# Decoder block on one core: TensorE's extra work folded into its loop, loads issued from a loop, heads in groups four apart

## The chip, the core and the metric

One core of one Trainium2 chip. A core has TensorE (PE), VectorE (DVE), ScalarE (ACT), GpSimd (POOL) and SyncE (SP); each runs its own program, and they wait for one another by semaphores. SP here does nothing but issue DMA transfers, which 16 DMA engines carry from the chip's memory (HBM) into the on-chip memory of 128 partitions. The metric is the device time of one execution in microseconds (us), the median of several. A profile is one execution seen by the hardware profiler; its span runs from the first to the last instruction.

## The reference

```python
def _A_ref(x, k_cache, v_cache, wq, wo):          # B, Sq, D = 4, 1, 512; H, Sk, Dh = 32, 4096, 128
    q = (x @ wq).reshape(B, Sq, H, Dh).transpose(0, 2, 1, 3)
    scores = jnp.einsum("bhqd,bhkd->bhqk", q, k_cache) * (Dh ** -0.5)
    p = _softmax(scores, axis=-1)
    o = jnp.einsum("bhqk,bhkd->bhqd", p, v_cache)
    return o.transpose(0, 2, 1, 3).reshape(B, Sq, H * Dh) @ wo
...
def _B_ref(x, w1, w2, w3, w4):                     # F = 1792
...
    x1 = x + hs
    h2 = _gelu(_layernorm(x1, axis=-1) @ w3) @ w4
    return x1 + h2
...
xn = _layernorm(x, axis=-1)
return x + _A_ref(xn, A_k_cache, A_v_cache, A_wq, A_wo) + _B_ref(xn, B_w1, B_w2, B_w3, B_w4)
```

With one position, every shift that builds `hs` moves zeros in, so `hs` is zero, `x1` is its input, and `w1` and `w2` are not read. What is left is attention of one query per head over 4096 cached keys and values (4 batches of 32 heads, float32), and a small MLP.

## The kernel before

K and V are 268 MB each and are read once. The 128 pairs of batch and head are cut into NG = 32 groups of HG = 4. A group's K is 8.39 MB: 128 partitions of 64 KB each, partition p holding 128 key rows of head p // 32 of the group. Before the change a group is four neighbouring heads, one contiguous stretch of memory:

```python
            def group(flat, g):
                n = HG * S * DH
                return flat[g * n:(g + 1) * n].rearrange("(p r) -> p r", p=P)
```

Three slots of 64 KB per partition hold everything large. K alternates between slot 1 (even groups) and slot 0 (odd groups); V has slot 2. Weights use the slots when they are free: wq lies in slot 2 at the start, the MLP's w3 and w4 in slot 2 at the end, wo in slot 0 at the very end. The last V group goes to slot 1.

Per group, four engines work one behind the other.

- DVE (L321 to L340) spreads the group's four queries into `qb`, waits for K, multiplies K by `qb` in two halves (L330, L332), sums the products to 128 scores per partition (L335), gives K's slot free (`k_free`), takes the maximum of each head (L337 to L340) and hands it to ACT (`d_a`).
- ACT (L238) takes exponentials into the tile `pw` and their sums into `rs`, and hands on to PE (`a_p`).
- PE waits for V (`s_v`) and for `pw`, runs 32 matmuls of `pw` with V (32 partitions by 512 columns into `pv`), one that sums `rs`, gives V's slot free (`v_free`), waits until ACT has copied `pv` to `os` (L244), and runs four small ones that collect the outputs into `oz`.
- SP keeps two orders: K of group g+2 behind `k_free` of group g (L119), V of group g+1 behind `v_free` of group g (L136), by turns, in one queue.

At the start x is loaded and normalised on DVE (to L308), PE multiplies it by wq with 32 matmuls, ACT scales the result, DVE transposes it (L316) and copies it to `Q` (L317). Then `d_T` lets SP issue K of group 1 and V of group 0. K of group 0 was issued right behind wq, in two halves (L123); a GpSimd relay passes the second half's arrival to DVE as `s_h`, and gives it 32 tokens at once, so that every turn of DVE's loop can take one.

SP's program has 65 loads written out. PE, ACT and DVE run loops over the groups. PE's and ACT's loops end before the last group, whose V is elsewhere: its turn, the MLP's first layer and the normalised outputs (`spread`: a matmul of a masked copy of each batch's outputs with a 0/1 matrix) are written out behind the loop. When the last reduce has freed slot 0, SP issues wo in six pieces (L148); PE multiplies each as it lands, 24 of the 32 row blocks into `y` and the last eight straight into `total`. Two copies and two stores of 4 rows end the program.

Of the kernel before, what the change touches and what calls it, by code (L numbers as in the profile page):

```python
# [7 lines left out]
F32 = mybir.dt.float32  # L8
AF = mybir.ActivationFunctionType
ALU = mybir.AluOpType  # L10
# [10 lines left out]
def decode_block(ctx: ExitStack, tc: tile.TileContext, x, k, v, wq, wo, w3, w4, out):  # L21
# [26 lines left out]
    X = sbuf("X", [P, WC, B])  # L48
# [3 lines left out]
    mask = sbuf("mask", [P, 4])  # L52
# [7 lines left out]
    ot = sbuf("ot", [P, JB, HG])  # L60
    rec = sbuf("rec", [P, JB, HG])
    lt = sbuf("lt", [P, H, 4])

    pv, oz, total, y, pa, pb = (nc.alloc_psum_tensor(f"ps{i}", [P, 512], F32) for i in range(6))
# [7 lines left out]
    PIECES = ((0, 8), (8, 16), (16, 24), (24, 28), (28, 31), (31, 32))  # L72
    CUT = 24
    s_x, s_v, s_vl, s_kh, s_h = (sem(n) for n in ("sx", "sv", "svl", "skh", "sh"))
    s_wq = [sem(f"swq{n}") for n in range(2)]
    s_k = [sem(f"sk{n}") for n in range(2)]
    s_wo = s_k + [s_v, s_x, s_kh, s_h]
    d_self, g_a, c_done, d_T, k_free, v_free = (sem(n) for n in ("dself", "ga", "cd", "dT", "kf", "vf"))
    d_a, a_d, p_a, a_p, d_p = (sem(n) for n in ("da", "ad", "pa", "ap", "dp"))

    kf = k.rearrange("b h s d -> (b h s d)")
    vf = v.rearrange("b h s d -> (b h s d)")
    out_r = out.rearrange("b s d -> (b s) d")

    def group(flat, g):
        n = HG * S * DH
        return flat[g * n:(g + 1) * n].rearrange("(p r) -> p r", p=P)
# [4 lines left out]
    q_sb = S0[:, 4 * D:6 * D].rearrange("p (n f) -> p n f", n=2)  # L92
    qT = S0[:, 6 * D:8 * D]
    xp = S0[:, 8 * D:8 * D + 2 * P].rearrange("p (e c i) -> p e c i", e=2, c=NC)
    xnT = S0[:, 9 * D:9 * D + P].rearrange("p (c m) -> p c m", c=NC)
    wq_sb = S2[:, :].rearrange("p (c n) -> p c n", c=NC)
    w3_sb = S2[:, :NC * F].rearrange("p (c f) -> p c f", c=NC)
    w34 = NC * F + NF * D
    w4_sb = S2[:, NC * F:w34].rearrange("p (m n) -> p m n", m=NF)
    hs, gu, gt, gT = (S2[:, w34 + n * FT:w34 + (n + 1) * FT] for n in range(4))  # L100
    V3 = S2[:, :].rearrange("p (c d) -> p c d", c=C)
    VL = S1[:, :].rearrange("p (c d) -> p c d", c=C)
# [10 lines left out]

    with tc.tile_critical(no_gpsimd_drain=True), nc.Block(no_gpsimd_drain=True) as block:

        @block.sync
        def _(e):
            def load_k(g):
                e.dma_start(KS[g % 2][:, :], group(kf, g)).then_inc(s_k[g % 2], 16)  # L119

            def load_k_half(g, n, s):
                r = slice(n * ROW // 2, (n + 1) * ROW // 2)
                e.dma_start(KS[g % 2][:, r], group(kf, g)[:, r]).then_inc(s, 16)  # L123

            wq_r = wq.rearrange("(p c) n -> p c n", p=P)
            for n in range(2):
                c = slice(n * NC // 2, (n + 1) * NC // 2)
                e.dma_start(wq_sb[:, c, :], wq_r[:, c, :]).then_inc(s_wq[n], 16)
# [12 lines left out]
            e.dma_start(S1[:, :], group(vf, NG - 1)).then_inc(s_vl, 16)  # L141
            take(e, v_free)
            e.dma_start(w3_sb, w3.rearrange("(p c) f -> p c f", p=P)).then_inc(s_wq[0], 16)
            e.dma_start(w4_sb, w4.rearrange("(p m) n -> p m n", p=P)).then_inc(s_wq[1], 16)
            take(e, k_free)
            wo_r = wo.rearrange("(p c) n -> p c n", p=P)
            for n, (c0, c1) in enumerate(PIECES):
                e.dma_start(wo_sb[:, c0:c1, :], wo_r[:, c0:c1, :]).then_inc(s_wo[n], 16)  # L148

        @block.gpsimd  # L150
        def _(e):
            e.memset(xs, 0.0).then_inc(g_a, 1)
            e.memset(ident[:, :], 0.0).then_inc(c_done, 1)
            e.memset(rs[:, :], 0.0)
            e.memset(pw[:, :, :], 0.0).then_inc(g_a, 1)
# [3 lines left out]
            take(e, s_kh, 16)  # L159
            e.wait_ge(c_done, 2).then_inc(s_h, NG)  # L160

        @block.tensor
        def _(e):
            def contract(V):
                for g in range(G4):
                    t = g % 4
                    i = mm(e, pv[32 * t:32 * t + 32, :], pw[:, g, :], V[:, 4 * g:4 * g + 4, :], g < 4, g >= G4 - 4)
                return i

            def outputs(done):  # L170
                i = mm(e, oz[:, HG:2 * HG], ones[:, :], rs[:, :], True, True)
                if done is not None:
                    i.then_inc(done, 1)
                take(e, a_p)
                for m in range(4):
                    i = mm(e, oz[:, 0:HG], os[:, m, :], sel[:, HG * m:HG * m + HG], m == 0, m == 3)
                i.then_inc(p_a, 1)

            def spread(b):
                take(e, d_p)  # L180
                mm(e, pa[:, 32 * b:32 * b + 32], lt[:, :, :], sel[:, :], True, True).then_inc(p_a, 1)

            e.wait_ge(d_T, 1)
            for c in range(NC):
                if c % (NC // 2) == 0:
                    take(e, s_wq[c // (NC // 2)], 16)
                w = wq_sb[:, c, :].rearrange("p (n j h d) -> p n h j d", n=2, j=JB // 2, h=HG)
                for n in range(2):
                    for h in range(HG):
                        i = mm(e, (pa, pb)[n][32 * h:32 * h + 32, :], xnT[:, c, :], w[:, n, h], c == 0, c == NC - 1)  # L190
                    if c == NC - 1:
                        i.then_inc(p_a, 1)

            with nc.Fori(0, NG - 1, 1, engines=[ET.PE]):
                take(e, s_v, 16)
                take(e, a_p)
                contract(V3).then_inc(p_a, 1)
                outputs(v_free)
            for b in range(B - 1):
                spread(b)  # L200
            take(e, a_p)
            take(e, s_vl, 16)
            contract(VL).then_inc(p_a, 1)
            e.wait_ge(s_wq[0], 16)
            for c in range(NC):
                for t in range(4):
                    i = mm(e, pb[32 * t:32 * t + 32, :FT], x1T[:, c, :], w3_sb[:, c, t * FT:(t + 1) * FT],
                           c == 0, c == NC - 1)
            i.then_inc(p_a, 1)
            outputs(None)  # L210
            spread(B - 1)
            mm(e, total[:, 0:P], ident[:, :], base[:, :], True, False)
            e.wait_ge(s_wq[1], 16)
            e.wait_ge(d_p, 1)
            for m in range(NF):
                t = m % 4
                mm(e, y[32 * t:32 * t + 32, :], gT[:, 32 * m:32 * m + 32], w4_sb[:, m, :], m < 4, False)

        @block.scalar
        def _(e):  # L220
# [5 lines left out]
            for n in range(2):  # L226
                take(e, p_a)
                e.mul(q_sb[:, n, :], (pa, pb)[n][:, :], DH ** -0.5).then_inc(a_d, 1)
            e.wait_ge(d_T, 2)
            e.activation(os[:, 0, 0:1], st[:, 3:4], AF.Exp)  # L230
            take(e, g_a)

            def weights():
# [6 lines left out]
                i.then_inc(a_p, 1)  # L240

            def outputs(o):
                take(e, p_a)
                e.copy(os[:, :, :], pv[:, :].rearrange("p (m d) -> p m d", m=4)).then_inc(a_p, 1)  # L244
# [3 lines left out]
            def spread(b):  # L248
                take(e, p_a)
                return e.copy(X[:, :, b], pa[:, 32 * b:32 * b + 32])  # L250

            with nc.Fori(0, NG - 1, 1, engines=[ET.Activation]) as g:
                weights()
                e.drain().then_inc(a_d, 1)
                outputs(OS[:, bass.ds(g, 1), :])
            weights()
            e.drain().then_inc(a_d, 1)
            for b in range(B - 1):
                spread(b).then_inc(c_done, 1)
            take(e, p_a)  # L260
            e.copy(os[:, :, :], pv[:, :].rearrange("p (m d) -> p m d", m=4)).then_inc(a_p, 1)
            take(e, p_a)
            e.copy(hs.rearrange("p (m i) -> p m i", i=32),
                   pb[:, :FT].rearrange("p (i m) -> p m i", i=32)).then_inc(a_d, 1)
# [159 lines left out]
```

## Time and profile before

| what | value |
|---|---|
| time, median of 3 (lowest to highest) | 1305.07 us (1304.78 to 1305.14) |
| the profiled execution's own time | 1304.94 us |
| its span | 1303.2 us |
| VectorE busy | 1169.3 us, 90% |
| TensorE matmuls busy | 364.8 us, 28% |
| ScalarE busy | 98.9 us, 8% |
| read from HBM | 561.00 MB, 430 GB/s over the span |
| TensorE's mean granted clock | 0.627 of full speed |

An engine's busy share tells which engines are far from a limit, not which one sets the time: the DMA queue is a resource of its own, with its own row. A part of the profile names, for each wait, what ended it; waits on semaphores that ran through the waiting engine's own sequencer appear there as "DVEq" or "PEq". A matmul in float32 appears as two records (x64 for 32 matmuls).

### The profile page before, as it was taken

What the parts mean: (1) busy time and instruction counts of PE and PEld (TensorE: products, weight loads), DVE (VectorE), ACT (ScalarE), POOL (GpSimd) and SP (SyncE); (2) the same over time, 40 slices, a digit from 0 to 9 for tenths busy, and PEclk for the clock granted to TensorE, in tenths of its full rate; (3) what the DMA queues carried; (4) which work ended last, traced back from release to release, by engine and by line L of the source; (5) the groups of instructions that cost most, each with busy time, mean ns of one, the idle gap of its engine ahead of it and who ended that gap; (6) DMA issues with size and microseconds to landing.
All of it is one profiled execution on the core that took longest, in us unless ns stands there. A gap on an engine that the chain in (4) does not pass through costs nothing. (4 is left out here: it accounts for less than half of the span.)

```text
span 1303.2 us, 7027 instructions
## 1 busy us (share of the span) xinstructions
PE 364.8 (28%) x2622; PEld 130.6 (10%) x2622; DVE 1169.3 (90%) x343; ACT 98.9 (8%) x335; POOL 2.1 (0%) x9
## 2 busy tenths in 40 slices
PE   2032123333113333213333212333311333321347
PEld 0010001111001111001111000111000111100112
DVE  4999999999999999999999999999999999999971
ACT  1000000000000000000000000000000000000010
POOL 0000000000000000000000000000000000000000
PEclk9565566666566666566666556666556666655669
DMA  9999999999999999999999999999999999999998
GB/s 403 435 447 422 447 420 449 420 447 422 430 437 424 445 422 447 422 447 422 447 420 449 421 447 422 439 428 428 441 422 447 422 445 424 445 424 445 422 429 347
DMA packets 10830, 561.08 MB, mean 431 GB/s; under 512 B 1212, under 2 KB 1220, under 8 KB 1480
## 3 DMA queue, kind: packets, MB, share of 16 engines
q1 hardware_dynamic: 10808, 561.00, 99.6%
q8 instruction: 3, 0.05, 0.0%
q14 instruction: 3, 0.02, 0.0%
q10 hardware_dynamic: 16, 0.01, 0.0%
HBM read 561.00 MB, written 0.01 MB: 430 GB/s over the span
## 5 line engine op out<-in xcount | busy, mean ns | idle before, releaser
L335 DVE TENSOR_REDUCE sc<-slot 128x128 f32<-128x16384 f32 x32 | 551.0, 17220 | 8.2 <-DVEq L70 8.2
L112 PE MATMUL ps<-slot,pw 128*32 128x512 f32 x2048 | 294.9, 740 | 882.2 <-PEq L70 882.2
L330 DVE TENSOR_TENSOR slot<-slot,qb 128x8192 f32<-128x8192 f32 x32 | 278.1, 8692 | 43.6 <-DVEq L70 43.6
L332 DVE TENSOR_TENSOR slot<-slot,qb 128x8192 f32<-128x8192 f32 x32 | 277.9, 8684 | 2.1 <-DVEq L70 2.1
L112 PEld LDWEIGHTS ps<-slot,pw 128*32 128x32 f32 x2048 | 80.7, 133 | 1071.0 <-issue 1070.9
L238 ACT ACTIVATE pw<-sc,st 32x128 f32<-32x128 f32 x128 | 67.3, 525 | 243.0 <-ACTq L70 241.5
L244 ACT COPY os<-ps 128x512 f32<-128x512 f32 x31 | 18.1, 585 | 857.1 <-ACTq L70 857.1
L112 PE MATMUL ps<-sel,os 128*128 128x4 f32 x256 | 32.8, 252 | 17.5 <-PEq L70 17.5
L112 PEld LDWEIGHTS ps<-sel,os 128*128 128x128 f32 x256 | 31.0, 191 | 19.3 <-issue 19.3
L238 ACT ACTIVATION_READ_ACCUMULATOR pw<-sc,st 32x1 f32 x128 | 26.1, 204 | 0.0
L112 PE MATMUL ps<-slot 128*32 128x512 f32 x92 | 14.0, 747 | 18.8 <-PEq L70 17.6
L327 DVE STREAM_TRANSPOSE qb<-qx 128x128 f32<-128x128 f32 x32 | 10.0, 311 | 4.9 <-DVEq L70 0.5
L386 DVE COPY res<-ps 64x128 f32<-64x128 f32 x1 | 0.3, 283 | 15.2 <-PE ps L112 15.2
L337 DVE TENSOR_REDUCE st<-sc 128x1 f32<-128x128 f32 x32 | 9.2, 286 | 4.7
L356 DVE TENSOR_TENSOR slot<-slot 128x448 f32<-128x448 f32 x1 | 0.6, 624 | 13.1 <-DVEq L70 13.1
L112 PE MATMUL ps<-rs,ones 128*128 128x4 f32 x64 | 12.3, 263 | 0.0
L112 PEld LDWEIGHTS ps<-rs,ones 128*128 128x128 f32 x64 | 9.5, 188 | 26.7 <-issue 26.7
L324 DVE COPY qx<-Q 128x128 f32 x32 | 7.3, 227 | 4.9 <-issue 4.6
L339 DVE STREAM_TRANSPOSE mt<-mx 128x32 f32<-128x32 f32 x32 | 6.8, 211 | 4.7
L340 DVE TENSOR_REDUCE st<-mt 128x1 f32<-128x32 f32 x32 | 6.0, 186 | 4.8 <-DVEq L70 1.8
L338 DVE COPY mx<-st 128x32 f32<-128x32 f32 x32 | 5.8, 181 | 4.7
L246 ACT COPY OS<-ps 128x8 f32 x31 | 5.1, 165 | 42.4 <-ACTq L70 42.4
(58 smaller groups left out, 54.2 us busy)
## 6 DMA issues: line engine op xcount, KB each, us to landing
slot<-in_A_wq_dram SPq DMA_DIRECT2D x2, 4096.0 KB, 16.8
slot<-in_A_k_cache_dram SPq DMA_DIRECT2D x2, 4096.0 KB, 35.8
slot<-in_B_w_dram SPq DMA_DIRECT2D x2, 3584.0 KB, 22.7
slot<-in_A_wo_dram SPq DMA_DIRECT2D x3, 2048.0 KB, 30.1
slot<-in_A_wo_dram SPq DMA_DIRECT2D x1, 1024.0 KB
slot<-in_A_wo_dram SPq DMA_DIRECT2D x1, 768.0 KB, 37.9
slot<-in_A_v_cache_dram SPq DMA_DIRECT2D x32, 28.8
slot<-in_A_k_cache_dram SPq DMA_DIRECT2D x31, 42.3
```

The costliest lines, as they stand in the source:

```text
L112: return e.matmul(o, l, r, start=start, stop=stop)
L238: i = e.activation(o, sc[r, :].rearrange("p (g w) -> p g w", w=4), AF.Exp, bias=st[r, 1:2], scale=1.0, accum_out=rs[r, h:h + 1])
L244: e.copy(os[:, :, :], pv[:, :].rearrange("p (m d) -> p m d", m=4)).then_inc(a_p, 1)
L324: own(e.tensor_copy(qx[:, :].rearrange("p (h r) -> p h r", h=4), Q[:, bass.ds(g + n, 1), :].rearrange("p o h -> p (o h)").unsqueeze(2) .to ...
L327: own(e.transpose(qb[:, :], qx[:, :]))
L330: e.tensor_tensor(out=K[:, :C // 2, :], in0=K[:, :C // 2, :], in1=qw, op=ALU.mult).then_inc(d_self, 1)
L332: e.tensor_tensor(out=K[:, C // 2:, :], in0=K[:, C // 2:, :], in1=qw, op=ALU.mult).then_inc(d_self, 1)
L335: e.reduce_sum(sc[:, :], K, axis=AX.X).then_inc(d_self, 1)
L337: own(e.reduce_max(st[:, 0:1], sc[:, :], axis=AX.X), 2)
L338: own(e.tensor_copy(mx[:, :], st[:, 0:1].to_broadcast([P, 32])))
L339: own(e.transpose(mt[:, :], mx[:, :]))
L340: e.tensor_reduce(st[:, 1:2], mt[:, :], axis=AX.X, op=ALU.max, negate=True).then_inc(d_a, 1)
```

## The change

Four things change, and the placement of TensorE's code.

1. **Heads and loads.** A group is now four heads that lie four apart (head 16n + 4t + e, for t = 0 to 3). Its K or V is four pieces of 2.1 MB, 8.4 MB apart in HBM; a load's source pattern counts 4, then 32, then 16384 elements, and its destination 128 partitions. SP's loads stand in a loop of eight turns with an address from a register.
2. **wq and the last group inside PE's loop.** wq is loaded like a V group into slot 2, and the loop's first of 33 turns multiplies it; DVE puts the normalised x into eight extra columns of `pw` for that. The last V group goes to slot 2 like the others, in two pieces (40 KB and 24 KB per partition); w3 and w4 go to slot 1 ahead of it. In every turn the last 12 matmuls of the 32 wait for a token of `v_rest`, which GpSimd gives out in the manner of `s_h` before.
3. **Outputs by a transpose.** DVE normalises 24 groups, then the last 8, and transposes them into `X`; the masked matmuls and their copies go. wo's rows are ordered to match (source pattern 4, then 32, then a piece of a row), and its pieces are 12, 8, 5, 3, 3 and 1 of 32.
4. **DVE's product** is one instruction over the whole of K, no longer two halves, and K of group 0 is one load.
5. **Code placement.** PE starts with a branch that, by a register, goes once to a block behind its loop and back.

```diff
-    PIECES = ((0, 8), (8, 16), (16, 24), (24, 28), (28, 31), (31, 32))
-    CUT = 24
+    PIECES = ((0, 12), (12, 20), (20, 25), (25, 28), (28, 31), (31, 32))
+    CUT = 28
+    GF = 20
...
+    NB = B * 2
+    kf = k.rearrange("b (n t e) s d -> (b n) e t (s d)", n=2, t=HG).rearrange("m e t (p r) -> m e t p r", p=32)
+    vf = v.rearrange("b (n t e) s d -> (b n) e t (s d)", n=2, t=HG).rearrange("m e t (p r) -> m e t p r", p=32)
...
+    nc.vector.addr_align(128, offset=100, max_nops=0)
+    turn = nc.alloc_registers("pe_turn_of_two", engines=[ET.PE])
+    nc.regs_mov(turn, 0)
...
-            for n in range(2):
-                c = slice(n * NC // 2, (n + 1) * NC // 2)
-                e.dma_start(wq_sb[:, c, :], wq_r[:, c, :]).then_inc(s_wq[n], 16)
-            load_k_half(0, 0, s_k[0])
-            load_k_half(0, 1, s_kh)
-            e.wait_ge(d_T, 2)
-            load_k(1)
-            for g in range(NG - 1):
-                if g > 0:
-                    take(e, v_free)
-                e.dma_start(S2[:, :], group(vf, g)).then_inc(s_v, 16)
-                if g + 2 < NG:
-                    take(e, k_free)
-                    load_k(g + 2)
+            def src(flat, m, i):
+                return flat[m, i] if isinstance(m, int) else flat[bass.ds(m, 1), i].rearrange("m t p r -> (m t) p r")
+            def load_k(m, i):
+                e.dma_start(KS[i % 2][:, :], src(kf, m, i)).then_inc(s_k[i % 2], 16)
+            def load_v(m, i):
+                take(e, v_free)
+                e.dma_start(S2[:, :], src(vf, m, i)).then_inc(s_v, 16)
+            FIRST, REST = slice(0, GF * 4 * DH), slice(GF * 4 * DH, ROW)
+            wq_r = wq.rearrange("(p c) n -> p (c n)", p=P)
+            e.dma_start(S2[:, FIRST], wq_r[:, FIRST]).then_inc(s_v, 16)
+            e.dma_start(S2[:, REST], wq_r[:, REST]).then_inc(s_q, 16)
+            load_k(0, 0)
+            e.wait_ge(d_T, 1)
+            load_k(0, 1)
+            with nc.Fori(0, NB, 1, engines=[ET.SP]) as m:
+                for i in range(3):
+                    load_v(m, i)
+                    take(e, k_free)
+                    if i < 2:
+                        load_k(m, i + 2)
...
-            e.dma_start(S1[:, :], group(vf, NG - 1)).then_inc(s_vl, 16)
-            take(e, v_free)
-            e.dma_start(w3_sb, w3.rearrange("(p c) f -> p c f", p=P)).then_inc(s_wq[0], 16)
-            e.dma_start(w4_sb, w4.rearrange("(p m) n -> p m n", p=P)).then_inc(s_wq[1], 16)
+            e.dma_start(w3_sb, w3.rearrange("(p c) f -> p c f", p=P)).then_inc(s_w3, 16)
+            e.dma_start(w4_sb, w4.rearrange("(p m) n -> p m n", p=P)).then_inc(s_w4, 16)
+            take(e, v_free)
+            last = src(vf, NB - 1, 3)
+            e.dma_start(S2[:, FIRST], last[:, :, FIRST]).then_inc(s_v, 16)
+            e.dma_start(S2[:, REST], last[:, :, REST]).then_inc(s_q, 16)
             take(e, k_free)
-            wo_r = wo.rearrange("(p c) n -> p c n", p=P)
+            wo_r = wo.rearrange("(h q c) n -> q h (c n)", h=H, q=4)
...
+            with nc.body("pe_top", valid_engines=pe):
+                e.br_lt(turn, 1, on_true="pe_far", on_false="pe_near")
+            with nc.body("pe_near", valid_engines=pe):
+                with nc.Fori(0, NG + 1, 1, engines=pe) as g:
+                    e.br_lt(g, NG, on_true="pe_turn", on_false="pe_mlp")
...
+                    take(e, s_v, 16)
+                    take(e, a_p)
+                    for n in range(G4):
+                        if n == GF:
+                            take(e, v_rest)
...
+                nc.br("pe_far", engines=pe)
+            with nc.body("pe_far", valid_engines=pe):
+                nc.regs_alu(turn, turn, 1, op=ALU.add)
+                e.br_lt(turn, 2, on_true="pe_top", on_false="pe_rest")
...
-                    e.tensor_tensor(out=K[:, :C // 2, :], in0=K[:, :C // 2, :], in1=qw, op=ALU.mult).then_inc(d_self, 1)
-                    take(e, s_h)
-                    e.tensor_tensor(out=K[:, C // 2:, :], in0=K[:, C // 2:, :], in1=qw, op=ALU.mult).then_inc(d_self, 1)
+                    own(e.tensor_tensor(out=K, in0=K, in1=qb[:, :].unsqueeze(1).to_broadcast([P, C, DH]), op=ALU.mult))
```

How the instructions stand, at three places. A row names the line, the operation, destination<-source, the destination's shape and the semaphores it waits for. **SP, from its first transfer**, before:

```order
L128 DMA slot<-in_A_wq_dram 128x8192 x2
L123 DMA slot<-in_A_k_cache_dram 128x8192 x2
L119 DMA slot<-in_A_k_cache_dram 128x16384 [waits dT]
L136 DMA slot<-in_A_v_cache_dram 128x16384
L119 DMA slot<-in_A_k_cache_dram 128x16384 [waits kf]
L136 DMA slot<-in_A_v_cache_dram 128x16384 [waits vf]
```

and now (the ISA rows work out addresses):

```order
L126 DMA slot<-in_A_wq_dram 128x10240
L127 DMA slot<-in_A_wq_dram 128x6144
L118 DMA slot<-in_A_k_cache_dram 128x1x16384
L118 DMA slot<-in_A_k_cache_dram 128x1x16384 [waits dT]
L131 UNCONDITIONAL_BRANCH
L122 ISA [waits vf]
L122 DMA slot<-in_A_v_cache_dram 128x1x16384
L118 ISA [waits kf]
L118 DMA slot<-in_A_k_cache_dram 128x1x16384
```

The order of K and V in the queue is the same; the first K is one load, the first V waits too, and a K or V load's destination carries a dimension of one because its source has one more than before. **SP, at the end of the groups**, before:

```order
L136 DMA slot<-in_A_v_cache_dram 128x16384 [waits vf]
L141 DMA slot<-in_A_v_cache_dram 128x16384 [waits kf]
L143 DMA slot<-in_B_w_dram 128x7168 [waits vf]
L144 DMA slot<-in_B_w_dram 128x7168
L148 DMA slot<-in_A_wo_dram 128x4096 [waits kf]
```

and now:

```order
L131 COMPARE_AND_BRANCH
L147 DMA slot<-in_B_w_dram 128x7168
L148 DMA slot<-in_B_w_dram 128x7168
L151 DMA slot<-in_A_v_cache_dram 128x1x10240 [waits vf]
L152 DMA slot<-in_A_v_cache_dram 128x1x6144
L156 DMA slot<-in_A_wo_dram 128x1x6144 [waits kf]
```

w3 and w4 have moved ahead of the last V group; the wait for `kf` that stood before that group's load is now the last one inside the loop. **PE, from its first matmul through one turn of its loop**, before:

```order
L112 MATMUL ps<-slot 32x512 [waits swq0,dT]
L112 MATMUL ps<-slot 32x512 x15
L112 MATMUL ps<-slot 32x512 [waits swq1]
L112 MATMUL ps<-slot 32x512 x15
L194 UNCONDITIONAL_BRANCH
L112 MATMUL ps<-slot,pw 32x512 [waits sv,ap]
L112 MATMUL ps<-slot,pw 32x512 x31
L112 MATMUL ps<-rs,ones 128x4
```

and now:

```order
L180 COMPARE_AND_BRANCH
L105 MATMUL ps<-slot,x1T 32x448 [waits sw3]
L105 MATMUL ps<-slot,x1T 32x448 x15
L188 UNCONDITIONAL_BRANCH
L105 MATMUL ps<-slot,pw 32x512 [waits sv,ap]
L105 MATMUL ps<-slot,pw 32x512 x19
L105 MATMUL ps<-slot,pw 32x512 [waits vr]
L105 MATMUL ps<-slot,pw 32x512 x11
L105 MATMUL ps<-rs,ones 128x4
```

The 32 matmuls with wq have gone into the loop's own 32; the MLP's 16 stand in the loop under a branch that only the last turn takes.

More of the change, by code (lines that the diff above doesn't have):

```diff
@@ L59, in decode_block @@
     res = sbuf("res", [2 * 32, 2, P])
[L60 to L64, printed above, removed]
+    ot = sbuf("ot", [P, B, H])
+    rec = sbuf("rec", [P, NG, HG])
+    warm = sbuf("warm", [P, 1])
+    pv, oz, total, y, pb = (nc.alloc_psum_tensor(f"ps{i}", [P, 512], F32) for i in range(5))
     def sem(name):
@@ new lines, in load_v @@
+            def load_v(m, i):
[11 more added lines that the diff above has]
+                    load_v(m, i)
+                    take(e, k_free)
+                    if i < 2:
+                        load_k(m, i + 2)
+                e.br_lt(m, NB - 1, on_true="sp_more", on_false="sp_next")
+                with nc.body("sp_more", valid_engines=[ET.SP]):
+                    after = nc.s_assert_within(m + 1, None, NB - 1,
+                                               skip_runtime_bounds_check_because="the last turn skips this block")
+                    load_k(after, 0)
+                    load_v(m, 3)
+                    take(e, k_free)
+                    load_k(after, 1)
+                    nc.br("sp_next", engines=[ET.SP])
+                nc.switch_bb("sp_next")
@@ L158, in _ @@
                             pattern=[[-1, P]], channel_multiplier=1).then_inc(c_done, 1)
-            take(e, s_kh, 16)
-            e.wait_ge(c_done, 2).then_inc(s_h, NG)
+            take(e, s_q, 16)
+            e.wait_ge(c_done, 2).then_inc(v_rest, NG)
+            take(e, s_q, 16)
+            e.wait_ge(c_done, 2).then_inc(v_rest, 1)
         @block.tensor
         def _(e):
[L164 to L168, printed above, removed]
@@ L183, in _ @@
[L183 to L192, printed above, removed]
@@ L194, in _ @@
[L194 to L217, printed above, removed]
+            pe = [ET.PE]
+            nc.br("pe_top", engines=pe)
+            with nc.body("pe_top", valid_engines=pe):
+                e.br_lt(turn, 1, on_true="pe_far", on_false="pe_near")
@@ L225, in _, with values @@
                 e.activation(st[:, 2:3], st[:, 1:2], AF.Sqrt, bias=st[:, 3:4], scale=1.0 / D).then_inc(a_d, 1)
-            for n in range(2):
+            def values():
                 take(e, p_a)
[L228 to L231, printed above, removed]
+                return e.copy(os[:, :, :], pv[:, :].rearrange("p (m d) -> p m d", m=4)).then_inc(a_p, 1)
+            values()
+            e.drain().then_inc(a_d, 1)
+            take(e, p_a)
+            e.activation(warm[:, :], st[:, 3:4], AF.Exp)
             def weights():
@@ L240, in weights @@
                 i.then_inc(a_p, 1)
+                e.drain().then_inc(a_d, 1)
             def outputs(o):
-                take(e, p_a)
-                e.copy(os[:, :, :], pv[:, :].rearrange("p (m d) -> p m d", m=4)).then_inc(a_p, 1)
+                values()
                 take(e, p_a)
                 return e.copy(o, oz[:, 0:2 * HG].unsqueeze(1))
[L248 to L252, printed above, removed]
+            act = [ET.Activation]
@@ L253, in _ @@
+            with nc.Fori(0, NG, 1, engines=act) as g:
                 weights()
-                e.drain().then_inc(a_d, 1)
+                e.br_lt(g, NG - 1, on_true="act_values", on_false="act_mlp")
+                with nc.body("act_mlp", valid_engines=act):
+                    take(e, p_a)
+                    e.copy(hs.rearrange("p (m i) -> p m i", i=32),
+                           pb[:, :FT].rearrange("p (i m) -> p m i", i=32)).then_inc(a_d, 1)
+                    take(e, d_a)
+                    e.activation(gt, gu, AF.Tanh, scale=GELU_A).then_inc(a_d, 1)
+                    nc.br("act_values", engines=act)
+                nc.switch_bb("act_values")
@@ L266, in _, with mark, own @@
-            e.copy(OS[:, NG - 1:NG, :], oz[:, 0:2 * HG].unsqueeze(1)).then_inc(a_d, 1)
-            e.wait_ge(d_a, 1)
-            e.activation(gt, gu, AF.Tanh, scale=GELU_A).then_inc(a_d, 1)
-            spread(B - 1)
         @block.vector
         def _(e):
-            def own(i, n=1):
+            done = [0]
+            def mark(i):
                 i.then_inc(d_self, 1)
-                take(e, d_self, n)
+                done[0] += 1
+            def own(i):
+                mark(i)
+                e.wait_ge(d_self, done[0])
@@ L277, in _, with clear, rows @@
+            def clear():
+                take(e, d_self, done[0])
+                done[0] = 0
+            def rows(t):
+                return slice(32 * t, 32 * t + 32)
             e.memset(ones[:, :], 1.0)
@@ L294, in layernorm, with transposed @@
                 own(e.reciprocal(st[:, 0:1], st[:, 2:3]))
[L296 to L299 removed]
+            def transposed(n, o):
                 for t in range(4):
```

164 lines of the change are left out of this document (75 added, 89 removed).

## The prediction

> **What bounds the kernel now.** I start with the page: its head, the DMA rows of the 40 slices and the queues.
>
> ```profile
> span 1303.2 us, 7027 instructions
> ...
> DMA  9999999999999999999999999999999999999998
> GB/s 403 435 447 422 447 420 449 420 447 422 430 437 424 445 422 447 422 447 422 447 420 449 421 447 422 439 428 428 441 422 447 422 445 424 445 424 445 422 429 347
> ...
> q1 hardware_dynamic: 10808, 561.00, 99.6%
> q8 instruction: 3, 0.05, 0.0%
> q14 instruction: 3, 0.02, 0.0%
> q10 hardware_dynamic: 16, 0.01, 0.0%
> ```
>
> The DMA engines are full in every slice, and SP's queue alone (q1) has 99.6% of their time. DVE, 90% busy, comes close, so the next view must say which of the two waits for the other. Two windows of the steady stretch (columns: window, its length, each engine's busy time, the granted clock, the DMA share, GB/s):
>
> ```profile
> 450.00:488.70 38.70, 11.18 (x74) 3.96 (x74) 35.91 (x9) 2.86 (x10) 0.00 (x0) 0.59 1.00 434
> ...
> 450.00:1224.10 774.10, 211.58 (x1480) 75.95 (x1480) 717.83 (x180) 57.15 (x200) 0.00 (x0) 0.62 1.00 433
> ```
>
> One group, K and V, is 16.78 MB, and at 433 GB/s takes 38.7 us; twenty groups take 774.1. DVE's rows in that stretch:
>
> ```profile
> 450.17 8.69 DVE L330 TENSOR_TENSOR slot<-slot,qb 128x8192 f32<-128x8192 f32 x1 [1.84 <-DVEq L70]
> 458.78 8.68 DVE L332 TENSOR_TENSOR slot<-slot,qb 128x8192 f32<-128x8192 f32 x1
> 467.72 17.22 DVE L335 TENSOR_REDUCE sc<-slot 128x128 f32<-128x16384 f32 x1 [0.26 <-DVEq L70]
> 485.09 0.29 DVE L337 TENSOR_REDUCE st<-sc 128x1 f32<-128x128 f32 x1
> 488.87 8.69 DVE L330 TENSOR_TENSOR slot<-slot,qb 128x8192 f32<-128x8192 f32 x1 [1.49 <-DVEq L70]
> ```
>
> and early in the program:
>
> ```profile
> 72.03 8.69 DVE L330 TENSOR_TENSOR slot<-slot,qb 128x8192 f32<-128x8192 f32 x1 [0.26 <-DVEq L70]
> ...
> 109.59 8.69 DVE L330 TENSOR_TENSOR slot<-slot,qb 128x8192 f32<-128x8192 f32 x1 [0.27 <-DVEq L70]
> ```
>
> Late, a turn takes 488.87 - 450.17 = 38.70 us, exactly the transfers' pace, and DVE idles 1.5 to 1.8 us ahead of it. Early, with 0.27 us of idle time, a turn takes 37.56 us. So DVE follows K, with some 1.1 us per turn to spare, and **the bytes set the time**: 561.00 MB at 433 GB/s are 1295.6 us, and 9.3 us of the profiled execution's 1304.94 lie around the stream. The chain that ended last says the same of the end:
>
> ```profile
> 1260.93 37.92 DMA slot<-in_A_wo_dram
> ...
> 1298.89 1.10 PE ps L112 x32
> ...
> 1300.02 0.28 DVE res L386
> ```
>
> The last of wo lands; 16 matmuls, a copy and the stores remain. The change can save time only in the 9.3 us, and cost time wherever it lets the queue run dry or slows a transfer.
>
> **The change, part by part.** *Bytes and transfers.* K and V 536.87 MB, wo and wq 8.39 each, w3 and w4 7.34: 561.00 MB as before. Loads to 128 partitions: before 2 of wq, 32 V, 2 + 31 of K, 2 of w3 and w4, 6 of wo, 75; after 2, 31 + 2, 32, 2, 6, again 75. The stream's price is unchanged, 0, as long as its pace is.
>
> *The start.* These rows of the timeline carry it:
>
> ```profile
> 0.96 0.87 SPq L128 DMA_DIRECT2D slot<-in_A_wq_dram  x2
> 1.88 1.01 SPq L123 DMA_DIRECT2D slot<-in_A_k_cache_dram  x2
> 17.19 0.31 DVE L308 STREAM_TRANSPOSE slot<-slot 128x128 f32<-128x128 f32 x1 [0.15 <-DVEq L70]
> 17.60 9.01 PE L112 MATMUL ps<-slot 128*32 128x512 f32 x64 [17.60 <-PEq L70]
> 27.50 1.25 DVE L316 STREAM_TRANSPOSE slot<-slot 128x1024 f32<-128x1024 f32 x1 [2.77 <-DVEq L70]
> 29.18 0.33 SPq L119 DMA_DIRECT2D slot<-in_A_k_cache_dram  x1
> 43.51 8.69 DVE L332 TENSOR_TENSOR slot<-slot,qb 128x8192 f32<-128x8192 f32 x1 [2.13 <-DVEq L70]
> ```
>
> After the transpose at 17.19 come two copies into `pw` (at most 0.3 us each, by that transpose of as many elements), then the same 32 matmuls, 9.01 us, one copy to `os` in place of two, a memset, a transpose half as wide as the 1.25 us one, and the scaling: `d_T` near 29.5, against 29.18. The queue holds wq and K of group 0, 16.78 MB, 38.7 us from about 2: it runs dry at 41. Some 11 us of cover; cost 0.
>
> *DVE's first product.* It no longer starts on half of K at 32.69 but on all of it, by 43.51 at the latest. Then 8.69 + 8.68 us of products end at 60.9, not 52.2: the turn ends 8.7 us later, and so do `k_free` and the third K load. The cover is V of group 0:
>
> ```profile
> 69.84 0.33 SPq L119 DMA_DIRECT2D slot<-in_A_k_cache_dram  x1
> ...
> 82.22 9.03 PE L112 MATMUL ps<-slot,pw 128*32 128x512 f32 x64 [55.61 <-PEq L70]
> ```
>
> PE's wait for that V ended at 82.22; the K load behind it will be issued at 69.84 + 8.7 = 78.5. That leaves 3.7 us. The nearest row for an issue's latency: the last store is issued at 1300.33 and the span ends at 1303.2, so issue, data and completion of a small transfer fit into 2.9 us. Bounds 0 to 2 us; I take 0. DVE then wins back 1.1 us per turn, and after some eight to twelve turns follows K again.
>
> *The loops.* `k_free` and `v_free` come from the same instructions, and the two orders alternate in the queue as before. Address arithmetic on SP stands behind a wait (an ISA row, tenths of a microsecond at most, by the 0.33 us issues); a load, once issued, queues far ahead of its need:
>
> ```profile
> slot<-in_A_v_cache_dram SPq DMA_DIRECT2D x32, 28.8
> slot<-in_A_k_cache_dram SPq DMA_DIRECT2D x31, 42.3
> ```
>
> A load of 8.39 MB takes 19.4 us of the stream, so V waits 9.4 us and K 23 us behind others. That covers the new token waits of `v_rest` too. Cost 0.
>
> *The end of the groups.*
>
> ```profile
> 1220.42 0.33 SPq L141 DMA_DIRECT2D slot<-in_A_v_cache_dram  x1
> 1243.71 8.55 PE L112 MATMUL ps<-slot,pw 128*32 128x512 f32 x64 [27.67 <-PEq L70]
> 1252.67 0.33 SPq L143 DMA_DIRECT2D slot<-in_B_w_dram  x1
> 1259.13 2.70 SPq L148 DMA_DIRECT2D slot<-in_A_wo_dram  x6
> 1284.96 4.96 PE L112 MATMUL ps<-slot 128*32 128x512 f32 x28 [1.19 <-DVE slot L363]
> 1291.06 5.37 PE L112 MATMUL ps<-slot,X 128*4 128x512 f32 x48 [1.13 <-SPq L365]
> ```
>
> From 1243.7 the queue carried V31 (19.4 us), w3 and w4 (17.0), wo. Now w3 and w4 take V31's issue time, 1220.42, and run until 1260.7; V31 is issued at 1252.67, 8 us ahead of that, and lands at 1280; wo is issued at 1259 for 1280. No gap. PE has 12 matmuls (12/32 of 8.55 us, 3.2), the copies and three small DVE operations left behind V31's second piece, some 6.5 us: 1286.5, while w4's 4.96 us of matmuls run beside them to 1290. wo's matmuls start near 1291, as before, and the last piece (one of 32, as before) sets the end. Bounds -0.5 to +0.5; I take 0.
>
> *Code placement.* The instruction rows are six packets of 0.07 MB. The longest, 0.05/3 MB on one of 16 engines at 27 GB/s, holds that engine 0.6 us, which counts only where it delays the last piece of wo. A jump at the start costs PE nothing while it idles to 17.60. Bounds -0.6 to +0.3; I take -0.1.
>
> Sum: 1304.94 - 0.1 = 1304.8 us, 0.3 under the median shown (1305.07), with 1303.3 to 1306.9 for this case alone.
>
> **The rivals.** *Four engines.* Where the pattern's slowest dimension counts four, the transfer may run on four DMA engines. The queue rows show such transfers. q1's 10808 packets are 75 loads of 128 rows and one store of 4: with 16 closing packets for each load and 4 for the store, 75 x (128 + 16) + (4 + 4) = 10808 exactly. q10's 16 are the load of x and the other store, 2 x (4 + 4). So 128 rows end on 16 engines, and 4 rows on four. A K or V load now has 128 partitions at its destination and 4 in front at its source. For 16: destination and size are those of the loads quoted, the nearest rows. For four: if the smaller count rules, all of K, V and wo, 545.26 MB, move at 4/16 of 433 GB/s, 108, in 5037 us; with wq's 19.4, a quarter-loaded 17.0 for w3 and w4 and the 9.3 around it, 5083 us, or 5240 at the lowest steady slice, 420. No row shows unequal counts, so this edit's price lies between 0 and +3900 us; I take 0, by the row nearest in size and destination, and give the other end 31%. [...]
>
> *A dry queue.* If the third K load comes later than V of group 0 is done, each microsecond late is one lost; the same if the four strided pieces of a load are read more slowly. It decides from 3.7 us of issue latency on, or a pace 0.3% lower: 1308 to 1330 us, 7%. Against it: 23 us of queueing before a K load in the steady state.
>
> *Faster than the bytes.* Only the 9.3 us around the stream can shrink, and 2.6 of them would have to go; the change there is of tenths. 3%. That the jump fetches nothing early is part of my forecast: it is worth at most 0.6 us.
>
> **How the numbers follow.** Forecast 59%: 1304.8 us. Four engines 31%, a dry queue 7%, faster 3%. A measurement of this kernel tells about 0.2%, 2.6 us, from no change: same 0.59, slower 0.31 + 0.07 = 0.38, faster 0.03. Leaving out the four engines would leave out more than 2 in 10, so the range reaches from 1303.3 to their upper bound, 5240.
>
> **What would show it.** Right: the DMA row full at 433 GB/s, V's issue to landing near 29 us, DVE's idle time before its product back at 1.5 us after a dozen turns, the end chain through wo's last piece. Four engines: a DMA share of 0.25, 108 GB/s, V and K landing after 78 us or more, DVE idle half its time or more. A dry queue: a slice below 420 GB/s near 80 us. The forecast is wrong if DVE's late first turn is still late at 500 us, or if the queue is full at a lower pace.

## The result, and the profile after

| | median | lowest to highest |
|---|---|---|
| before | 1304.96 us | 1304.78 to 1305.35 |
| changed | 5487.45 us | 5466.48 to 6589.55 |
| ratio | 4.202 | 95% interval 4.1945 to 4.2096 |

The change made the kernel four times slower. The forecast of 1304.8 us was wrong, and the rival with four engines had the right mechanism at too low a price (5083 to 5240 us).

The profile beside these times fell on the slowest execution, 6589.55 us, which the ratio leaves out and in which the slower pace described below lasted until about 4900 us; so the lines below are those of a second profile of the same kernel, whose own time was 5475.51 us. The head of its page, the DMA rows of the 40 slices, and SP's queue:

```profile
span 5473.6 us, 6995 instructions
...
DMA  3222222222222222222222222222222222222421
GB/s 109 59 64 68 76 89 102 105 98 106 108 108 109 108 108 109 107 109 109 108 109 108 108 109 108 108 109 108 109 109 107 109 108 108 109 108 108 134 84 77
...
q1 hardware_dynamic: 9956, 560.99, 25.6%
```

The bytes are those of before, 560.99 MB, and one queue still carries them. But the DMA row is a quarter full where it was full. The packets say why. The kernel makes 75 loads, 65 of them of K and V. With 16 closing packets for the four loads of wq, w3 and w4, four for each of the other 71 loads, and four for the store, there are 64 + 284 + 4 = 352, beside 75 x 128 + 4 = 9604 of data: 9956 exactly. All K, V and wo loads ended on four engines.

Five windows of the same profile (columns as in the prediction: window, length, busy times, clock, DMA share, GB/s):

```profile
0.00:100.00 100.00, 11.01 (x74) 3.84 (x74) 14.17 (x40) 3.94 (x6) 2.09 (x9) 0.66 0.40 128
100.00:1300.00 1200.00, 53.10 (x370) 18.97 (x370) 231.02 (x49) 16.38 (x58) 0.00 (x0) 0.52 0.25 83
1300.00:5080.00 3780.00, 262.57 (x1828) 93.78 (x1832) 879.37 (x200) 68.55 (x240) 0.00 (x0) 0.53 0.25 108
5080.00:5255.00 175.00, 12.82 (x103) 5.08 (x95) 35.31 (x6) 3.44 (x11) 0.00 (x0) 0.53 0.39 124
5255.00:5470.00 215.00, 32.21 (x235) 9.31 (x234) 5.33 (x12) 4.77 (x14) 0.00 (x0) 0.57 0.22 79
```

The steady pace is 108 GB/s, a quarter of 433, at a share of 0.25: four engines, each as fast as before. Two stretches are slower: the one from 100 to 1300 us, at 83 GB/s with the same share, and the end, where the last V group and wo move at 79. DVE, 90% busy before, now mostly waits for K. Its product's row in the costliest groups (the last numbers are the idle time ahead of it):

```profile
L334 DVE TENSOR_TENSOR slot<-slot,qb 128x16384 f32<-128x16384 f32 x32 | 551.2, 17225 | 4008.9 <-DVEq L69 4008.9
```

The end of the chain of waits (start, length, what):

```profile
5255.10 0.53 SPq L156
...
5255.67 75.81 SPq L156
5331.48 0.04 issue
5331.52 47.20 SPq L156
...
5379.34 57.47 SPq L156
...
5436.85 32.88 DMA slot<-in_A_wo_dram
```

SP itself now stands on the chain: single issues of wo take 47 to 76 us, where all six took 2.70 before.

### The profile page after: what moved, and what is told of

Its sections match the earlier page's. It is cut to its first block, busy times and chain, and to the rows that moved or that the text cites. A ratio compares the mean times of both kernels' runs of the same rounds, so it can differ in the third digit from the quotient of the medians.

```text
span 6587.7 us, 6995 instructions
## 1 busy us (share of the span) xinstructions
PE 368.2 (6%) x2600; PEld 130.0 (2%) x2600; DVE 1165.4 (18%) x307; ACT 97.3 (1%) x330; POOL 2.1 (0%) x9
## 3 DMA queue, kind: packets, MB, share of 16 engines
q1 hardware_dynamic: 9956, 560.99, 25.3%
## 5 line engine op out<-in xcount | busy, mean ns | idle before, releaser
L334 DVE TENSOR_TENSOR slot<-slot,qb 128x16384 f32<-128x16384 f32 x32 | 551.2, 17225 | 5120.3 <-DVEq L69 5120.3
```

The lines of the kernel that those rows point to most:

```text
L334: own(e.tensor_tensor(out=K, in0=K, in1=qb[:, :].unsqueeze(1).to_broadcast([P, C, DH]), op=ALU.mult))
```

## The experiments

Each edit is against the changed kernel unless another is named. Where no spread is given, the time is that of one execution.

**Heads next to each other.** Only the order of the heads goes back; loops, register addresses, the end and wo's loads stay.

```diff
-    kf = k.rearrange("b (n t e) s d -> (b n) e t (s d)", n=2, t=HG)...
+    kf = k.rearrange("b (n e t) s d -> (b n) e t (s d)", n=2, t=HG)...
```

(and the same for `vf`.)

> The changed kernel, but a group's four heads are neighbours again in HBM (queries and keys are then paired otherwise than in the reference); a K or V load's source then merges to one count of 128. Theory, the smaller of the two outermost counts sets the number of DMA engines: K and V go back to 16 engines, only wo stays on four, 8.39 MB in 77 us in place of 19, so 1305 + 58 = 1363 us. Rival, loads from a loop with an address from a register are slow in themselves: no change, about 5480 us. Rival, heads 8.4 MB apart are read slowly by any number of engines: about 1305 us, and not settled by this run.

Measured: 1395.03 us. Its windows over the groups, and over wo:

```profile
100.00:1240.00 1140.00, 302.95 (x2146) 109.21 (x2146) 1070.51 (x240) 85.02 (x298) 0.00 (x0) 0.61 1.00 433
1260.00:1389.00 129.00, 26.36 (x192) 7.61 (x192) 5.42 (x13) 4.55 (x13) 0.00 (x0) 0.61 0.34 125
```

With neighbouring heads the source's 4 and 32 merge into one count of 128, and K and V are back at 433 GB/s. The packets of SP's queue agree: 10736 are 9604 of data, 16 closings for each of 69 loads, and four for each of wo's six and for the store. So neither SP's loop nor the addresses from a register slow a load. What is left, 90 us, is wo, whose source still counts 4, then 32; it was dearer than expected by 32 us.

**Each load cut in four**, of 32 partitions each, with heads four apart as in the change. Both sides now count 32.

```diff
+            def four(dst, s, sm):
+                for t in range(4):
+                    e.dma_start(dst[32 * t:32 * t + 32], s[t]).then_inc(sm, 16)
...
-                e.dma_start(KS[i % 2][:, :], src(kf, m, i)).then_inc(s_k[i % 2], 16)
+                four(KS[i % 2][:, :], src(kf, m, i), s_k[i % 2])
```

> The changed kernel with the same heads four apart, but each load cut into four of 32 partitions, one for each head; each then counts 32 on both sides. Theory of the counts: 16 engines again, 1300 to 1400 us, though four times as many issues. Rival, heads 8.4 MB apart are read slowly: above 2000 us, as addresses and bytes are the same. Rival of the loop: about 5480 us or more.

Measured: 2699.51 us. A window of it:

```profile
200.00:2500.00 2300.00, 293.00 (x2072) 106.43 (x2072) 1026.02 (x226) 80.01 (x280) 0.00 (x0) 0.55 1.00 207
```

All 16 engines are busy again (share 1.00), but at half the pace. So the count explains the number of engines, and something else halves the pace of all 16. The time missed the theory's 1300 to 1400 us and lies where the rival of slowly read addresses had put it; the run on neighbouring heads in four loads, further down, decides between the two. The trace's records give 5.07 us for a packet of 64 KB, where the kernel before has 2.42.

**Each load cut in two**, of 64 partitions, with a source count of 2.

```diff
+            def two(dst, s, sm):
+                for t in (0, 2):
+                    e.dma_start(dst[32 * t:32 * t + 64, :], s[t:t + 2]).then_inc(sm, 16)
```

> The changed kernel with each K and V load cut into two of 64 partitions, two heads each, which count 2 at their source. Theory of the counts: two engines, half the pace of the changed kernel: 534 MB at 50 to 54 GB/s, 9900 to 10700 us, and a DMA share of about 0.13. Any rival by addresses, loop or size of a transfer: about 5480 us or less, since nothing else is worse than before.

Measured: 10439.97 us. SP's queue, then two windows:

```profile
q1 hardware_dynamic: 9972, 560.99, 13.2%
```

```profile
100.00:500.00 400.00, 0.00 (x0) 0.00 (x0) 35.79 (x8) 2.11 (x8) 0.00 (x0) 0.50 0.13 28
...
1500.00:5000.00 3500.00, 123.00 (x860) 44.39 (x852) 393.99 (x88) 34.29 (x120) 0.00 (x0) 0.51 0.13 54
```

Two engines of sixteen are a share of 0.125, and the pace is an eighth of 433. With the bytes and addresses of the changed kernel, half the count gave half the pace. The number of loads is not what decides: four loads of 32 partitions, twice as many again, ran on 16 engines.

**Repaired**: loops, the end and the jump of the change, but neighbouring heads (V's rows and `pw` read with strides so that the outputs come out in the same order) and wo's pieces as four loads of 32 partitions.

```diff
-                e.dma_start(wo_sb[:, c0:c1, :], wo_r[:, :, c0 * D:c1 * D]).then_inc(s_wo[n], 16)
+                for q in range(4):
+                    e.dma_start(wo_sb[32 * q:32 * q + 32, c0:c1, :].rearrange("p c n -> p (c n)"),
+                                wo_r[q, :, c0 * D:c1 * D]).then_inc(s_wo[n], 16)
```

> The changed kernel with its loops and its code placement, but K and V loaded as neighbouring heads (one count of 128); the rows of V or wq that a matmul takes are four apart instead, so that the result is the reference's; and each wo piece is four loads of 32 partitions. Theory of the counts: everything on 16 engines, 1305 us plus or minus 3, that is the rest of the change costs and gains nothing that can be measured. Rival, part of the slowdown comes from the loop, the first product over the whole of K or PE's jump: 1320 us or more.

Measured: 1324.47 us (1323.31 to 1325.72), ratio 1.0149 [1.0132, 1.0166]. Two windows:

```profile
100.00:1260.00 1160.00, 319.01 (x2252) 115.06 (x2252) 1090.06 (x245) 95.32 (x300) 0.00 (x0) 0.62 1.00 433
1260.00:1322.00 62.00, 31.08 (x200) 8.30 (x200) 5.52 (x13) 5.13 (x14) 0.00 (x0) 0.69 0.89 257
```

The groups run as before, at 433 GB/s. The 19.5 us more lie at the end: wo's 8.39 MB take 19.4 us at 433 GB/s, and 39 to 41 us at the 206 and 215 GB/s that the profile shows for its 32-partition loads from 1280 to 1290 and from 1290 to 1300 us. The time missed 1305 plus or minus 3 and lies where the rival of loop, product and jump had put it, 1320 or more; wo in rows, further down, keeps those three and has none of the loss.

**Where the half pace comes from: the destination or the addresses.** The repaired kernel with K, V, wq and the last V group in four loads of 32 partitions, from neighbouring heads (`four` as above).

> Neighbouring heads again, in the form of the repaired kernel, but every K and V load (and wq and the last V group) is cut into four loads of 32 partitions, as in four_loads. If the half pace of four_loads comes from the destination (all 16 engines writing the same 32 partitions at a time), the queue stays full at about 207 GB/s and 64 KB packets take about 5.1 us: 2690 to 2720 us. If it comes from the addresses four apart, the pace is that of before, 433 GB/s, and only wo stays slow: 1320 to 1335 us.

Measured: 2696.3 us.

```profile
200.00:2500.00 2300.00, 296.52 (x2072) 106.34 (x2072) 1029.69 (x226) 88.86 (x280) 0.00 (x0) 0.55 1.00 207
```

The same 207 GB/s from contiguous memory: the addresses four apart are cleared. What the two slow runs still share is that a load is a quarter as large and goes to 32 neighbouring partitions; the next two runs tell these apart.

**Which property of the destination.** Two kernels, equal but for one slice, on neighbouring heads with wo in rows (the kernel further down); each K and V load (and the first pieces of wq and of the last V group) is cut into two of 64 partitions. The diff is that of halves; even and odd has `slice(h, P, 2)` in its place.

```diff
+                for h in range(2):
+                    r = slice(64 * h, 64 * h + 64)
+                    e.dma_start(KS[i % 2][r, :], src(kf, m, i)[r, :]).then_inc(s_k[i % 2], 16)
```

> Neighbouring heads, wo in loads of 128 partitions, and each K and V load (and the first pieces of wq and of the last V group) cut into two: partitions 0 to 63 and 64 to 127, with equal counts of 64 on both sides. If the half pace of 32-partition loads comes from the share of partitions that a load reaches, 64 partitions run at full pace or between: 1305 to 1700 us. If pairs of engines meet at places that partitions 32 apart share (a packet takes 5.1 us beside another and 2.42 us alone), the first 64 partitions offer no more places than 32, and the pace is again about 207 GB/s: 2620 to 2700 us.

> As near_halves, but the two loads take the even and the odd partitions, so each load spreads over all 128. If only the number of partitions in a load counts, it runs like near_halves. [...]

Measured: halves 2662.39 us, even and odd 1305.89 us. A window of halves, then one of even and odd:

```profile
200.00:2400.00 2200.00, 283.69 (x1998) 102.91 (x1998) 983.78 (x217) 85.72 (x270) 0.00 (x0) 0.55 1.00 207
```

```profile
200.00:1240.00 1040.00, 284.81 (x1998) 102.13 (x1990) 971.98 (x217) 85.80 (x270) 0.00 (x0) 0.61 1.00 433
```

Loads of 64 partitions run at half pace, 207 GB/s, if they are 0 to 63 and 64 to 127, and at full pace, 433 GB/s, if they are every other one. So it is neither the number of partitions nor the size of a load. And 64 neighbours got no more than 32 did, 207 GB/s both times. In halves the trace's 8064 packets of 64 KB have a mean of 5.06 us, in even and odd of 2.42: a little over twice as long. The time of halves lies in the 2620 to 2700 us that one of its two cases gave, but the meeting of engines in that case was the author's guess, and no run shows it. Nor is 2.42 us the length of a packet alone: the kernel before has it at a DMA share of 1.00.

**Heads three apart**, for the missing pace of the four engines.

```diff
-                return flat[m, i] if isinstance(m, int) else flat[bass.ds(m, 1), i].rearrange("m t p r -> (m t) p r")
+                return flat[m, i % 3] if isinstance(m, int) else flat[bass.ds(m, 1), i % 3].rearrange("m t p r -> (m t) p r")
```

(with `kf` and `vf` cut so that 12 heads give three groups of four.)

> The changed kernel with a group's four heads three apart (6.3 MB) in place of four apart (8.4 MB); it reads 96 of the 128 heads, some of them twice, so the outputs are of other heads. The source still counts 4, then 32. If unequal counts alone decide, four engines carry the data as in the changed kernel, 5.1 to 5.5 ms. If four engines lose their last 8% (100 GB/s in place of 4 x 27.1) because the four heads lie a power of two apart, this runs at about 108 GB/s: 5060 to 5120 us. If the loss has another cause, 5450 to 5500 us. If the distance of 8.4 MB itself were the cause of the whole loss, about 1310 to 1400 us.

Measured: 5490.55 us. Two windows:

```profile
100.00:1000.00 900.00, 31.32 (x222) 11.33 (x222) 167.20 (x34) 10.67 (x38) 0.00 (x0) 0.52 0.25 76
1000.00:2000.00 1000.00, 73.50 (x518) 26.48 (x518) 226.79 (x55) 19.99 (x70) 0.00 (x0) 0.53 0.25 109
```

The slow start is there at 6.3 MB too: that the heads lie a power of two apart is not its cause.

**The kernel before with only the loads of K and V four apart.**

```diff
-        return flat[g * n:(g + 1) * n].rearrange("(p r) -> p r", p=P)
+        return flat[g // 4, g % 4]
```

> The kernel before with one edit: the loads of K and V take the heads four apart, with the source pattern that counts 4, then 32, and nothing else of the change. Its outputs pair queries with other heads' keys. If the loads' counts are the whole of the result, four engines carry 537 MB and wo's six loads keep 16: 5250 to 5500 us, and less than the changed kernel by wo's share, some 60 to 190 us. If the loops, the register addresses or the order at the end have a part in it, it is clearly less.

Measured: 5322.03 us, 4017 more than the kernel before beside it (1304.8).

```profile
100.00:1000.00 900.00, 43.22 (x294) 15.26 (x295) 177.15 (x45) 11.27 (x39) 0.00 (x0) 0.52 0.25 82
1000.00:2000.00 1000.00, 62.64 (x448) 22.80 (x447) 221.93 (x55) 19.42 (x69) 0.00 (x0) 0.53 0.25 108
```

One edit of the change, alone, brings 96% of the loss (4017 of 5475.51 - 1304.8 = 4171 us, by one execution of each); the other 153 us are within what was expected for wo.

**The changed kernel once more**, the profile shown above.

> The changed kernel itself, for a profile beside the others: 5460 to 5500 us, a DMA share of 0.25, about 100 GB/s as a mean over the groups.

Measured: 5475.51 us, a share of 0.25, and 108 GB/s over most of the groups with 83 from 100 to 1300 us.

**wo in rows.** The repaired kernel with wo's loads as before the change, on 128 partitions of equal counts, and one matmul that brings the outputs into wo's order; and the same without TensorE's jump.

```diff
-            wo_r = wo.rearrange("(h q c) n -> q h (c n)", h=H, q=4)
+            wo_r = wo.rearrange("(p c) n -> p c n", p=P)
...
+                e.dma_start(wo_sb[:, c0:c1, :], wo_r[:, c0:c1, :]).then_inc(s_wo[n], 16)
...
+            e.tensor_copy(perm[:, :].rearrange("p (h q) -> p h q", q=4), ident[:, :].rearrange("p (q h) -> p h q", q=4))
...
+        mm(e, pb[:, 0:P], perm[:, :], X[:, :, :].rearrange("p b h -> p (b h)"), True, True).then_inc(x_p, 1)
+        nc.vector.wait_ge(x_p, 1)
+        nc.vector.tensor_copy(ot[:, :, :].rearrange("p b h -> p (b h)"), pb[:, 0:P]).then_inc(p_x, 1)
```

> The repaired kernel with wo back in loads of 128 partitions with equal counts, as before the change; a matmul with a permuted identity brings the transposed outputs into wo's order. Everything else of the change stays: loops, the order at the end, the product in one piece, PE's jump. If the loads' forms are the whole of the loss, wo takes 19.4 us again in place of 39: 1304.0 to 1305.8 us, the same as before within 0.2%. If the loops or the end cost something that wo's slow loads hid in the repaired kernel, 1307 us or more.

> wo_in_rows without TensorE's jump into the block behind its loop and back, and nothing else changed. If the jump does nothing on the path, as forecast (0 to 0.6 us), the two agree within 0.6 us; if it fetches code early that the end needs, this one is 0.6 us or more slower than wo_in_rows.

Measured: wo in rows 1305.62 us (1305.20 to 1306.52), ratio to before 1.0006 [0.9997, 1.0015]; without the jump 1305.69 us, ratio 1.0007 [0.9998, 1.0016]. SP's rows of the timeline in the first (start, length):

```profile
29.42 0.33 SPq L120 DMA_DIRECT2D slot<-in_A_k_cache_dram  x1
30.17 0.35 SPq L124 DMA_DIRECT2D slot<-in_A_v_cache_dram  x1
78.54 0.34 SPq L120 DMA_DIRECT2D slot<-in_A_k_cache_dram  x1
...
1252.95 0.33 SPq L153 DMA_DIRECT2D slot<-in_A_v_cache_dram  x1
...
1259.17 2.70 SPq L158 DMA_DIRECT2D slot<-in_A_wo_dram  x6
```

its windows around the third K load:

```profile
70.00:80.00 10.00, 0.00 (x0) 0.00 (x0) 9.61 (x7) 0.49 (x2) 0.00 (x0) 0.50 1.00 433
80.00:90.00 10.00, 7.49 (x52) 2.19 (x56) 9.98 (x1) 1.94 (x8) 0.00 (x0) 0.67 0.99 406
90.00:100.00 10.00, 2.90 (x26) 1.53 (x18) 9.87 (x2) 0.75 (x2) 0.00 (x0) 0.84 1.05 452
```

and DVE's product in the first two turns and later (idle time ahead of it in brackets):

```profile
43.68 17.23 DVE L336 TENSOR_TENSOR slot<-slot,qb 128x16384 f32<-128x16384 f32 x1 [13.36 <-DVEq L70]
...
80.02 17.23 DVE L336 TENSOR_TENSOR slot<-slot,qb 128x16384 f32<-128x16384 f32 x1
...
372.97 17.23 DVE L336 TENSOR_TENSOR slot<-slot,qb 128x16384 f32<-128x16384 f32 x1 [0.80 <-DVEq L70]
...
450.38 17.22 DVE L336 TENSOR_TENSOR slot<-slot,qb 128x16384 f32<-128x16384 f32 x1 [2.50 <-DVEq L70]
489.08 17.23 DVE L336 TENSOR_TENSOR slot<-slot,qb 128x16384 f32<-128x16384 f32 x1 [2.12 <-DVEq L70]
```

The two agree with each other, and no difference from the kernel before can be told. With the loads' forms put right, the rest of the change neither costs nor saves what this measurement can see, and no version here beats the kernel before.

## Why the prediction was wrong

**The bound was right.** The bytes set the time before, and the transfers set it after: DVE's work is the same and waits 4009 us.

**The step that failed** is the price of unequal counts: "this edit's price lies between 0 and +3900 us; I take 0, by the row nearest in size and destination". The runs showed +4171 us in its place, 4017 of them from the K and V loads' pattern alone: four engines, a DMA share of 0.25 and 108 GB/s. The nearest row in size was not the nearest in what decides. The packet counts had just shown that 4 rows end on four engines and 128 on sixteen (4 and 16 closing packets), and the edit put a 4 in front of one side. The number of engines followed the smaller count: 4 against 128 gave four engines (a DMA share of 0.25), 2 against 64 two (0.13), and equal counts of 128, 64 or 32 sixteen (1.00). What other unequal counts give, no run here shows.

**The rival's size was too low**: 5083 us against 5475.5 in the profiled execution, 392 short, and the range's upper end, 5240, was 247 under the median. Its term "4/16 of 433 GB/s, 108" holds in the steady part only. From 100 to 1300 us the pace was 83, which is 1200 x (1 - 83/108) = 278 us; in the last stretch 79, which is 215 x (1 - 79/108) = 58 us. Behind the start, too, the pace was low:

```profile
22.00:100.00 78.00, 6.26 (x54) 2.48 (x46) 2.68 (x9) 2.07 (x3) 0.00 (x0) 0.57 0.26 57
```

It cost 78 x (1 - 57/108) = 37 us. The remaining 19 us I have put down to no place. The 420 GB/s slice behind my upper end said how 16 engines vary, not how four do.

**The other steps** can be read in wo in rows, which keeps all of the change but the two load patterns, and adds one matmul and one copy.

- *The start*: the K load behind `d_T` was issued at 29.42 us; near 29.5 was forecast.
- *DVE's first product*: the third K load came at 78.54 us; 78.5 was forecast. The queue did not run dry: from 70 to 100 us it moved 433, 406 and 452 GB/s at a share of about 1. The 406 is under the 420 that the forecast had named as a sign, but the three windows have a mean of 430, and the kernel before moved 419, 500 and 433 in the same ones. The rival of the dry queue falls.
- *The loops*: 433 GB/s over the groups. DVE won back its late start, and by more per turn than I took: its first turns took 36.3 to 36.8 us (80.02 - 43.68 = 36.34), no longer 37.56, so later 2.1 to 2.5 us of a 38.70 us turn are idle, not 1.1. It followed K again from 372.97 us, its tenth product, within the eight to twelve turns of the forecast, but by luck: at 38.70 us per turn, its second product should have begun at 372.97 - 8 x 38.70 = 63.4 us to be in step, and it began at 80.02, some 17 us late. The forecast had counted only the 8.7 us that the change adds, not the lag that the kernel before has already (its second product began at 72.03, in place of some 63), and only half of what a turn wins back. Behind the transfers this is worth nothing.
- *The end of the groups*: the last V load was issued at 1252.95 us and wo at 1259.17; 1252.67 and 1259 were forecast.
- *The jump*: forecast -0.1 us; with and without it 1305.62 and 1305.69 us, a difference inside either's spread.

The time that these steps gave, 1304.8 us, was that of the kernel without its two load patterns, to within 0.1%. The range given for this case alone, 1303.3 to 1306.9, is not the sum of the bounds of its terms, which is 1303.8 to 1307.7; 1305.62 lies in both.

## What to carry to other kernels

Before a load's pattern is changed, write down the counts that the transfer carries on both sides, after dimensions that follow each other have merged (the 4 and 32 of neighbouring heads ended on 16 engines, at 433 GB/s): here a leading 4 against 128 meant four engines, and it is the DMA share of the profile that shows it (0.25), not the GB/s alone. If a load must be cut to get equal counts, its parts should still spread over the partitions: 32 or 64 adjacent ones ran at half pace, 207 GB/s, with every engine busy (a share of 1.00), every other one at full pace, 433 GB/s. When a bound has two ends four times apart, ask which row is nearest in the quantity that decides, not in size.

## What the runs showed of the hardware

- **Full but slow.** A DMA share of 1.00 went with 433 and with 207 GB/s, so the share is no measure of the pace; a packet's duration tells them apart (2.42 against 5.06 us for 64 KB).
- **Four engines, and two, started slowly.** Four moved 76 to 83 GB/s over about the first 1000 us and then 108; two moved 28 from 100 to 500 us and 54 from 1500. All engines of the transfer were busy throughout (shares of 0.25 and 0.13), and it is the packets that were slower: in the changed kernel's trace, those of 64 KB that began between 100 and 500 us took 4.20 us in the mean (2.42 to 5.13), those between 1300 and 5080 us 2.42. No run shows what made them slower, or what ends the slow stretch.
- **SP's issue stalled.** In the changed kernel single issues of wo held SP for up to 76 us, and the next one began 0.04 us after; with neighbouring heads, where wo alone ran on four engines, for up to 84 us, and with the loads cut in two for up to 74. It need not be the stalled load's own pattern: in the changed kernel w4, with equal counts, took 6.97 us to issue behind V's loads, and w3, just ahead of it, 0.33. And an issue of a K or V load took 0.55 us with four engines and three counts, 0.33 with sixteen and neighbouring heads; no run tells which of the two it is.
